# Which second-layer groups lead each chunk of a fused attention and two-layer kernel, and when two additions follow the fifth product

## The chip, the cores and the metric

The kernel runs on one core of a Trainium2 chip. The metric is the device time of one execution in microseconds (us), lower is better. The time before is 329.29 us, the median of three runs (327.78 to 329.35).

## The reference

Causal attention over 8 batches, 8 heads, 576 queries of 64 elements, with 16 additional "beacon" keys that every query sees, and then two dense layers over the 4608 tokens with a leaky ReLU between them:

```
scores = q @ concat(beacon_k, k).T / 8      # queries see only earlier keys, and all beacons
a = exp(scores - max); a /= a.sum()
x = (a @ concat(beacon_v, v)) as [4608, 512]
h = x @ w_in            # [4608, 2048]
g = maximum(0.01 * h, h)
out = g @ w_out         # [4608, 512]
```

## The kernel before

**Attention** goes by pairs of heads, 32 pairs g = 0 to 31, four to a batch. Pairs 0 to 7 are written out by hand as strings of steps. From pair 8 on, `load_natural` (step N, L167) has POOL load q and k, `turn_pair` (step T, L177) has SP issue two transposing DMAs for them, and a `block` (L787) computes 1536 columns of scores: `stretch` (L299) writes them into two one-bank tiles and two two-bank tiles of PSUM, and ACT reads each with Exp (L329, L333) into `aT`. POOL zeroes the triangles (L289). `value` (L374) multiplies by v on PE (L359), in half 0 (12 matmuls) and half 1 (18), and DVE divides by the sums (L388, L389) into `x_nat`. `x_turn` (L412) has SP issue two transposing DMAs that put the pair's 128 columns into `xT`, the input of the first layer.

**The two layers** go by nine chunks of 512 tokens. A first-layer group (`up`, L630, and `moe1`, L431) makes 128 of the 2048 hidden columns of a chunk: four matmuls of 512 columns (L442), one for each quarter j of the 512 inputs; j = 3 needs the last pair of a batch. ACT reads the result with Prelu (L450) into `gT`. There are 16 such groups for a chunk. A second-layer group (`down`, L642, and `moe2`, L524) is eight matmuls of 256 columns (L537). Chunk 0 takes 16 plain groups (L512); each later chunk takes seven products in the order 1, 4, 6, 2, 7, 5, 3 (a Strassen scheme), each in two groups that share a PSUM bank, 14 groups in all. The sums of hidden blocks that products 6, 5 and 3 read are made by DVE (`token_sums`, L469, issued one to a group at L621). After a product's second group, `combine` (L556) reads the bank: ACT copies products 1, 4 and 5 (L568), DVE adds the others (L565), and `store` (L591) has SP send finished blocks out.

In this text **u2.0** is first-layer group 0 of chunk 2, **d1.12** is second-layer group 12 of chunk 1, and **block 7** is the call of `block` with m = 7. The groups d.10 and d.11 of a chunk are product 5; d.12 and d.13 are product 3, the last.

**The order** on each engine is the order in which the Python code issues; nothing reorders it. From pair 8 on a list of events (blocks, values, transposes, loads) is walked in order, and between events `fill` (L603) issues groups, up or down in turn, until the count of groups issued reaches an aim that is spread evenly over the batch. KEPT = 4 groups are held back from each batch's aim, so that four second-layer groups of the old chunk are left when a batch's last pair arrives. At that point `finish` (L685) sets `held` to LEAD = 2: the next two groups are second-layer ones, and they run while the DMA brings the last pair's columns of `xT`. The other two are kept back by the condition with LAST = 2 in `fill`: as long as only two second-layer groups of the chunk are left, first-layer groups go first. With values and blocks left in, the order before around chunk 2 is

```
d1.8 d1.9 d1.10 [value 12, half 1] [x_turn 12] d1.11 (additions of product 5) u2.0 [block 7] u2.1 u2.2 u2.3 [value 13, half 0] u2.4 u2.5 ...
... u2.14 [block 9] u2.15 d1.12 d1.13 [value 15, half 0] d2.0 d2.1 [value 15, half 1] d2.2 ...
```

and around chunk 3

```
d2.10 [block 11] d2.11 (additions of product 5) d2.12 [value 16, half 1] u3.0 u3.1 u3.2 [value 17, half 0] u3.3 u3.4 [block 12] u3.5 d2.13 u3.6 ...
```

Chunks 5 and 6 repeat these two patterns (blocks 20 to 22 and 24 to 25).

**Additions of product 5.** `combine` for product 5 copies the bank by ACT into `p5` and puts two DVE additions and a store into the list `late`. `add_late` (L552), called at the start of every group, issues all that is in the list: so they stand on DVE's queue from the next group on.

**PSUM.** Four of the eight banks form the pool `ps_one` (banks 4 to 7), shared by first-layer groups, products, values and the two one-bank tiles of each block. A bank is given on as soon as its reader is done.

Of the kernel before, what the change touches and what calls it, by code (L numbers as in the profile page):

```python
# [15 lines left out]
def kernel(  # L16
# [487 lines left out]
    def ND(i):  # L504
        return NF if i == 0 else 2 * len(PRODUCTS)
# [18 lines left out]
    def moe2(i, n2):  # L524
        if i == 0:
            moe2_plain(i, n2 // 4, n2 % 4)
            if n2 == NF - 1:
                weight_sums(1)
            return
        n, tile = PRODUCTS[n2 // 2], n2 % 2  # L530
        apart = i == NCH - 1 and n2 >= 10
        if tile == 0 or apart:
            banks["p"] = ps_one.tile([128, 512], FP32, name="acc", tag="one")
        acc = banks["p"]
        lo = 0 if apart else tile * HD
        for fc in range(HF):
            nc.tensor.matmul(  # L537
                out=acc[:, lo : lo + HD],
                lhsT=left(i, n, fc, tile),
                rhs=right(n, fc),  # L540
                start=(lo == 0 and fc == 0),
                stop=(fc == HF - 1),
                skip_group_check=True,
            )
        if apart:
            combine(i, n, acc[:, 0:HD], (tile, tile + 1))
        elif tile == 1:
            combine(i, n, acc, (0, 2))

    late = []  # L550

    def add_late():  # L552
        while late:
            late.pop(0)()

    def combine(i, n, acc, tiles):  # L556
        lo, hi = tiles[0] * HD, tiles[1] * HD

        def part(name, new=False):
            if new and lo == 0:  # L560
                parts[name] = opool.tile([128, 512], FP32, name=name, bufs=1)
            return parts[name][:, lo:hi]

        def add(to, x, y):
            nc.vector.tensor_tensor(out=to, in0=x, in1=y, op=ADD)  # L565

        if n in (1, 4, 5):
            nc.scalar.copy(out=part(f"p{n}", True), in_=acc)  # L568
        if n == 6:
            add(part("u2", True), acc, part("p1"))  # L570
        elif n == 2:
            add(part("p1"), acc, part("p1"))
            store(i, 0, 0, tiles, part("p1"))
        elif n == 7:
            add(part("u3", True), acc, part("u2"))
            add(part("p4"), part("u3"), part("p4"))
            store(i, 1, 0, tiles, part("p4"))
        elif n == 5:
            u2, u3, p5 = part("u2"), part("u3"), part("p5")

            def rest():
                add(u3, u3, p5)
                store(i, 1, 1, tiles, u3)
                add(p5, u2, p5)

            late.append(rest)
        elif n == 3:
            add(part("p5"), acc, part("p5"))
            store(i, 0, 1, tiles, part("p5"))

    def store(i, half, cols, tiles, c):  # L591
        t0 = i * 512 + half * HT + tiles[0] * 128
        n = tiles[1] - tiles[0]
        nc.sync.dma_start(
            out=out[t0 : t0 + n * 128, cols * HD : (cols + 1) * HD].rearrange("(t p) d -> p t d", p=128),
            in_=c.rearrange("p (t d) -> p t d", t=n),
        )

    done1, done2, at2, ready, turn, first_down, held = [0], [0], [0, 0], [0], [0], [0], [0]

    LAST = 2

    def fill(rest=False):  # L603
        i1, fc = divmod(done1[0], NF)
        i2, n2 = at2
        can1 = i1 < ready[0] and (i1 < 2 or i2 > i1 - 2)
        can2 = i2 < NCH and i2 < i1 and done1[0] >= first_down[0]
        if held[0] and can2:
            held[0] -= 1
            down()  # L610
        elif can1 and not (rest and can2) and (turn[0] == 0 or not can2 or (i1 == i2 + 1 and ND(i2) - n2 <= LAST)):
            up()
        elif can2:
            down()
        return can1 or can2
# [14 lines left out]
    def up():  # L630
        i1, n = divmod(done1[0], NF)
        assert i1 < ready[0]
        add_late()
        fc = n if i1 == 0 else n // 2 + n % 2 * HF
        moe1(i1, fc)
        add_due()
        done1[0] += 1
        turn[0] = 1
        if i1 and n % (2 * SLICE) == 2 * SLICE - 1:
            due.extend((i1, op) for op in token_sums(i1, n // 2 + 1 - SLICE, n // 2 + 1))  # L640

    def down():  # L642
        add_late()
        add_due()
        if at2[1] == 4:
            add_all(at2[0])
        moe2(*at2)
        done2[0] += 1
        at2[1] += 1
        if at2[1] == ND(at2[0]):  # L650
            at2[:] = at2[0] + 1, 0
        turn[0] = 0
# [19 lines left out]
            )  # L672

    NG = B * NPAIR
    KEPT, LEAD = 4, 2

    def has(g):
        return 0 <= g < NG
# [68 lines left out]
    with order:  # L747
# [76 lines left out]
        for at, _, what, args in events:  # L824
            while w + 2 < len(ends) and at > ends[w + 1]:
                w, d0 = w + 1, done1[0] + done2[0]
            todo = NF * ready[0] + sum(ND(i) for i in range(ready[0])) - KEPT - d0
            aim = d0 + todo * (at - ends[w]) / (ends[w + 1] - ends[w])
            while done1[0] + done2[0] < aim and fill():
                pass  # L830
            if what is block:
                since = done1[0] + done2[0]
            elif what is value:
                while done1[0] + done2[0] < since + (2 if has_down() else 4) and fill(True):
                    pass
            what(*args)
        while at2[0] < NCH:
            fill()
# [30 lines left out]
```

## Time and profile before

| | us |
|---|---|
| median of three runs | 329.29 |
| lowest and highest | 327.78, 329.35 |
| the profiled execution, its own time | 334.47 |
| span of that execution in the trace | 332.7 |
| PE busy with matmuls | 322.6 |
| ACT busy | 200.7 |
| POOL busy | 185.6 |
| DVE busy | 145.6 |
| 16 DMA engines, mean moved | 120 GB/s |

The profile shows one execution. The profiled one took 334.47 us, 1.77 us of it outside the traced span, and is 5.18 us longer than the median; so times from the trace are compared with the trace's own span. A row of the timeline has the start, the time to the end of the last instruction of the row, the engine (PE matmul, PEld weight load, DVE, ACT, POOL, and SPq for SP's issue of DMAs), the line of the kernel, the operation, output and inputs with shapes, the count, and in brackets the engine's idle time just before and what ended it. Matmuls overlap in the pipeline, so that what counts on PE is the distance from start to start.

### The profile page before, as it was taken

The numbers are of one execution on the slowest core, as the hardware profiler recorded it, in microseconds if no ns is written. First come the engines' busy times: TensorE is split into PE (matmuls) and PEld (weight loads), VectorE is DVE, ScalarE is ACT, GpSimd is POOL, SyncE is SP. The second block draws the span as 40 slices with busy tenths as digits, with TensorE's granted clock in tenths as the row PEclk, the third lists the DMA queues.
The fourth block names the chain that finished last, engine by engine and source line by source line (L and its number), as shares of the span: only waits on it lengthen the run. The fifth ranks groups of instructions, "written<-read, shape, count | busy, mean of one in ns | idle before, by whom it ended". The sixth has DMA issues, their size and how long they took to land.

```text
span 332.7 us, 8488 instructions
## 1 busy us (share of the span) xinstructions
PE 322.6 (97%) x3401; PEld 215.7 (65%) x3429; DVE 145.6 (44%) x297; ACT 200.7 (60%) x336; POOL 185.6 (56%) x354
## 2 busy tenths in 40 slices
PE   8999999999999899999999999999999999999995
PEld 5457456445587457855688888656865695566685
DVE  3327245713565154534434535543553552424344
ACT  3657986197864785477756785686467516643510
POOL 8847874999998568656966887667221000000000
PEclk9999999999999999999999999999999999999999
DMA  7999999999999999999999999999521111000203
GB/s 128 139 181 173 114 195 142 149 179 177 141 140 141 194 133 106 160 145 124 118 138 197 137 146 102 189 106 121 98 97 51 36 52 64 2 33 30 66 32 128
DMA packets 155928, 39.93 MB, mean 120 GB/s; under 512 B 143040, under 2 KB 153152, under 8 KB 155888
## 3 DMA queue, kind: packets, MB, share of 16 engines
q0 software_dynamic: 99824, 18.54, 82.8%
q1 hardware_dynamic: 55792, 20.77, 36.8%
q8 instruction: 27, 0.44, 0.6%
q14 instruction: 13, 0.11, 0.2%
q10 hardware_dynamic: 272, 0.07, 0.1%
HBM read 37.22 MB, written 9.44 MB: 140 GB/s over the span
## 4 chain that ended last, share of the span: by engine, by line
PE 86%; ACT 5%; DMA 4%; DVE 2%; issue 2%; SPq 1%; DVEq 0%; ACTq 0%; POOLq 0%
PE acc L442 34%; PE acc L537 26%; PE av L359 8%; PE sc L314 6%; PE acc L512 4%; PE sc L267 3%; ACT aT L333 3%; DMA xT<-x_nat 2%; PE tp L243 2%; PE av L658 2%; DMA gsum<-in_q_dram 1%; DVE u L565 1%; DVE p L565 1%; ACT aT L329 1%; ACT gT L450 1%
## 5 line engine op out<-in xcount | busy, mean ns | idle before, releaser
L442 PE MATMUL acc<-xT,w_in_sb 128*128 128x512 bf16 (+1 forms) x616 | 134.8, 357 | 3.8 <-DMA xT<-x_nat 1.9
L450 ACT ACTIVATE gT<-acc 128x512 bf16<-128x512 f32 x144 | 83.6, 616 | 54.9 <-PE acc L442 51.1
L289 POOL TENSOR_SCALAR_AFFINE_SELECT aT<-aT 128x256 bf16<-128x256 bf16 (+2 forms) x160 | 61.8, 415 | 66.7 <-ACT aT L329 33.5
L442 PEld LDWEIGHTS <-w_in_sb 128*128 128x128 bf16 x640 | 59.5, 98 | 54.3 <-issue 4.5
L537 PEld LDWEIGHTS <-gT 128*128 128x128 bf16 x512 | 48.8, 98 | 8.3 <-issue 1.2
L333 ACT ACTIVATE aT<-sc 128x1024 bf16<-128x1024 f32 (+3 forms) x64 | 51.8, 896 | 0.0
L537 PE MATMUL acc<-w_out_sb,gT 128*128 128x256 bf16 x384 | 46.2, 273 | 0.1
L359 PEld LDWEIGHTS <-aT 128*128 128x128 bf16 (+1 forms) x960 | 36.8, 98 | 9.0 <-issue 2.6
L537 PEld LDWEIGHTS <-gsum 128*128 128x128 bf16 x384 | 36.8, 98 | 6.7
L359 PE MATMUL av<-v_aug,aT 128*128 128x65 bf16 (+1 forms) x960 | 39.5, 195 | 1.0 <-DVE x_nat L389 0.7
L329 ACT ACTIVATE aT<-sc 128x512 bf16<-128x512 f32 (+3 forms) x64 | 29.0, 522 | 17.9 <-PE sc L314 17.9
L568 ACT COPY p<-acc 128x512 f32<-128x512 f32 (+1 forms) x25 | 14.5, 581 | 38.8 <-PE acc L537 35.2
L388 DVE RECIPROCAL rec<-av 128x6 f32<-128x6 f32 (+1 forms) x64 | 12.0, 187 | 57.9 <-PE av L359 57.6
L171 POOL DMA_DIRECT2D k_nat<-in_k_dram x48 | 34.8, 732 | 0.4
L171 POOL DMA_DIRECT2D q_nat<-in_q_dram x48 | 34.8, 729 | 0.5 <-issue 0.3
L214 POOL DMA_DIRECT2D v_aug<-in_v_dram x40 | 34.2, 858 | 0.2 <-DMA gsum<-in_q_dram 0.2
L389 DVE TENSOR_TENSOR x_nat<-av,rec 128x384 bf16<-128x384 f32 (+1 forms) x64 | 31.4, 491 | 2.2
L276 ACT ACTIVATE aT<-sc 128x1024 bf16<-128x1024 f32 (+3 forms) x32 | 26.7, 875 | 8.8 <-PE sc L267 8.5
L537 PE MATMUL acc<-w_sum,gsum 128*128 128x256 bf16 x256 | 31.9, 273 | 0.0
L621 DVE TENSOR_TENSOR gsum<-gT 128x1024 bf16<-128x1024 bf16 x16 | 11.1, 693 | 30.1 <-ACT gT L450 30.1
L314 PE MATMUL sc<-qT,kT 64*128 64x80 bf16 (+22 forms) x384 | 21.9, 250 | 0.0
L314 PEld LDWEIGHTS <-kT 64*128 64x128 bf16 x384 | 12.8, 94 | 11.6 <-issue 8.1
(62 smaller groups left out, 234.3 us busy)
## 6 DMA issues: line engine op xcount, KB each, us to landing
out_dram<-p SPq DMA_DIRECT2D x26, 256.0 KB, 3.3
q_nat<-in_q_dram POOLq DMA_DIRECT2D x48, 72.0 KB, 5.5
k_nat<-in_k_dram POOLq DMA_DIRECT2D x48, 72.0 KB, 5.3
v_aug<-in_v_dram POOLq DMA_DIRECT2D x24, 128.0 KB, 6.5
w_in_sb<-in_moe_w_in_dram POOLq DMA_DIRECT2D x2, 1024.0 KB, 10.1
w_out_sb<-in_moe_w_out_dram POOLq DMA_DIRECT2D x2, 1024.0 KB, 10.8
out_dram<-u SPq DMA_DIRECT2D x8, 256.0 KB, 3.1
gsum<-in_q_dram POOLq DMA_DIRECT2D x8, 144.0 KB, 5.3
```

Source lines behind the costliest of these rows:

```text
L171: nc.gpsimd.dma_start(out=t[:, :, par], in_=(q, k)[which][b, 2 * hp + par].rearrange("(t p) d -> p t d", p=NR),)
L214: nc.gpsimd.dma_start(out=dst[lo : ROWS[c], c, :, 0:D], in_=v[b, :, OFF[c] : OFF[c] + n].rearrange("h p d -> p h d"),)
L276: nc.scalar.activation(out=aT[:, :, c0 : c0 + w], in_=sc[:, :, 0:w], func=AF.Exp, scale=0.125)
L289: nc.gpsimd.affine_select(out=view, in_=view, compare_op=ALU.is_ge, fill=0.0, base=128 - n if lo == 0 else 0, channel_multiplier=-1, patte ...
L314: nc.tensor.matmul(out=(sc[par] if apart else sc[:, par])[:, at : at + b - a], lhsT=kT[ps_, c * 128 : (c + 1) * 128], rhs=qT[ps_, q0 : q0 ...
L329: nc.scalar.activation(out=probs[g][:, par, lo:hi], in_=sc[par][:, at : at + hi - lo], func=AF.Exp, scale=0.125)
L333: nc.scalar.activation(out=probs[g][:, :, lo:hi], in_=sc[:, :, at : at + hi - lo], func=AF.Exp, scale=0.125)
L359: nc.tensor.matmul(out=avv[:, n, 0 : D + 1], lhsT=aT[0 : ROWS[c], par, a0 : a0 + 128], rhs=va[0 : ROWS[c], c, 2 * hp + par, :], start=(c = ...
L389: nc.vector.tensor_tensor(out=x_nat[:, t0:t1].rearrange("p t e d -> p (t e) d"), in0=avv[:, :, 0:D], in1=rec[:, n0:n1, None].to_broadcast( ...
L442: nc.tensor.matmul(out=acc[:, lo:hi], lhsT=w_in_cols(fc, j), rhs=xT[:, j, x0 : x0 + hi - lo], start=(j == 0), stop=(j == NJ - 1), skip_gro ...
L450: nc.scalar.activation(out=gT[i][:, fc, :], in_=acc, func=AF.Prelu, alpha=0.01)
L537: nc.tensor.matmul(out=acc[:, lo : lo + HD], lhsT=left(i, n, fc, tile), rhs=right(n, fc), start=(lo == 0 and fc == 0), stop=(fc == HF - 1) ...
```

## The change

`LEAD` becomes 4, the same as `KEPT`, so that all four second-layer groups that are left go ahead of the next chunk's first layer. The condition with `LAST` is removed from `fill`. An entry of `late` carries a count of groups, and `add_late` issues it only once that count has passed, which is two groups after the copy instead of one; the last product's `combine` forces what is left, since it adds to the same buffer.

```diff
-    def add_late():
-        while late:
-            late.pop(0)()
+    def add_late(now=False):
+        while late and (now or late[0][0] < done1[0] + done2[0]):
+            late.pop(0)[1]()
...
-            late.append(rest)
+            late.append((done1[0] + done2[0] + 1, rest))
         elif n == 3:
+            add_late(True)
             add(part("p5"), acc, part("p5"))
             store(i, 0, 1, tiles, part("p5"))
...
-
-    LAST = 2
...
-        elif can1 and not (rest and can2) and (turn[0] == 0 or not can2 or (i1 == i2 + 1 and ND(i2) - n2 <= LAST)):
+        elif can1 and not (rest and can2) and (turn[0] == 0 or not can2):
             up()
...
-    KEPT, LEAD = 4, 2
+    KEPT, LEAD = 4, 4
```

The order after it around chunk 2 is

```
d1.8 d1.9 d1.10 [value 12, half 1] [x_turn 12] d1.11 d1.12 [block 7] (additions of product 5) d1.13 u2.0 u2.1 u2.2 [value 13, half 0] u2.3 ...
... u2.12 [block 9] u2.13 u2.14 u2.15 [value 15, half 0] d2.0 d2.1 [value 15, half 1] d2.2 ...
```

and around chunk 3

```
d2.10 [block 11] d2.11 d2.12 [value 16, half 1] (additions of product 5) d2.13 u3.0 u3.1 [value 17, half 0] u3.2 u3.3 [block 12] u3.4 ...
```

The instructions are the same in kind and number. POOL's order is the same. SP's differs in the places of a few stores, and DVE's and ACT's in the places of the additions, sums, copies and Prelus that belong to moved groups.

## The prediction

> **What bounds the kernel now.** I read the busy shares first, then the PE waits, then the PE timeline from start to start around each chunk's beginning.
>
> ```profile
> PE 322.6 (97%) x3401; PEld 215.7 (65%) x3429; DVE 145.6 (44%) x297; ACT 200.7 (60%) x336; POOL 185.6 (56%) x354
> ...
> DMA  7999999999999999999999999999521111000203
> ```
>
> PE is the bound, and the DMA engines are nearly as full until about 230 us. PE's own waits between 80 and 300 us are few:
>
> ```profile
> PE acc L442 <- DMA xT<-x_nat: 1.9, 1, 1.9
> PE av L359 <- DVE x_nat L389: 0.7, 2, 0.4
> PE acc L442 <- ACT gT L450: 0.4, 2, 0.2
> ```
>
> They understate the loss, since a row's end overlaps the next row. From start to start a 512-column matmul takes 0.216 us (12 in 2.59 us), a 256-column one 0.109 (16 in 1.74), so a group takes 0.87 us; value half 0 takes 0.37, half 1 0.56, a block 0.77. What exceeds these is lost time. Around chunk 2's start:
>
> ```profile
> 106.58 0.81 PE L442 MATMUL acc<-xT,w_in_sb 128*128 128x512 bf16 x3
> 109.33 0.38 PE L442 MATMUL acc<-xT,w_in_sb 128*128 128x512 bf16 x1 [1.93 <-DMA xT<-x_nat]
> 109.64 0.83 PE L314 MATMUL sc<-qT,kT 64*128 64x272 bf16 x16
> 110.40 2.77 PE L442 MATMUL acc<-xT,w_in_sb 128*128 128x512 bf16 x11
> 113.00 0.53 PE L359 MATMUL av<-v_aug,aT 128*128 128x65 bf16 x12
> 113.75 2.53 PE L442 MATMUL acc<-xT,w_in_sb 128*128 128x512 bf16 x11 [0.21 <-ACT gT L450]
> ```
>
> u2.0 does three matmuls (0.65 us) and waits for the fourth's columns of xT: 109.33 - 106.58 - 0.65 = **2.10 us** lost. Later, value 13's 12 matmuls take 0.75 instead of 0.37: **0.38** lost, for a bank. ACT shows why:
>
> ```profile
> 109.74 0.60 ACT L450 ACTIVATE gT<-acc 128x512 bf16<-128x512 f32 x1 [2.37 <-PE acc L442]
> 110.23 1.08 ACT L329 ACTIVATE aT<-sc 128x512 bf16<-128x512 f32 x2
> 111.19 2.02 ACT L333 ACTIVATE aT<-sc 128x768 bf16<-128x768 f32 x3
> 113.04 2.37 ACT L450 ACTIVATE gT<-acc 128x512 bf16<-128x512 f32 x4
> ```
>
> The Prelus of the groups behind a block stand behind the block's Exps. Block 7 starts at 109.64; the first Prelu behind it starts 3.40 us later, and PE goes on with its bank at 113.75, 4.1 us behind the block's start; the next follow at a pitch of 0.5 us. With four banks, whatever PE allocates fifth behind a block waits until then. Chunk 5's start repeats the 0.38 (value 25 at 214.82). Chunk 3's start:
>
> ```profile
> 144.14 2.80 PE L442 MATMUL acc<-xT,w_in_sb 128*128 128x512 bf16 x11
> 147.30 0.53 PE L359 MATMUL av<-v_aug,aT 128*128 128x65 bf16 x12 [0.35 <-DVE x_nat L389]
> ```
>
> and DVE in the same stretch:
>
> ```profile
> 145.04 0.84 DVE L565 TENSOR_TENSOR u<-u,p 128x512 f32<-128x512 f32 x1 [3.27 <-ACT p L568]
> 145.91 0.69 DVE L565 TENSOR_TENSOR p<-u,p 128x512 f32<-128x512 f32 x1
> 146.52 0.17 DVE L388 RECIPROCAL rec<-av 128x4 f32<-128x4 f32 x1
> ```
>
> Twelve matmuls (one record is missing) take 147.30 - 144.14 = 3.16 instead of 2.60: **0.56** lost. The two additions of product 5 wait for ACT's copy, which stands behind block 11's Exps, and hold up value 16's division, whose bank value 17 needs; d2.12's bank is idle until d2.13. Chunk 6's start repeats it (245.97 to 249.12, 0.55).
>
> **What the Trainium skill says.** "Perfetto Trace Analysis", section Identifying the Most-Contended Engine: matmul busy share is a poor measure of headroom. The trace agrees: PE reads 97% and these places still lose 2.10 + 2 x 0.38 + 0.56 + 0.55 = 3.97 us. Its section Optimization Strategy takes a repeated gap as a sign that there may be too few PSUM buffers for the next tile; the 0.38 and the 0.56, each seen twice, are such. "TensorE: Matmul & The Clock Gate", Back-to-back issue gap, gives 518 cycles for 512 columns at 2.4 GHz, 0.216 us, as measured. "PSUM — Partial Sum Buffer", Engine vs sequencer instructions: ScalarE's and VectorE's queues are strictly first in, first out. The rows above agree.
>
> **The change part by part.**
>
> *Four groups lead.* At chunk 2's start d1.12 (106.58 to 107.45), block 7 (to 108.2) and d1.13 (to 109.1) now stand ahead of u2.0. Its fourth matmul is due at 109.1 + 0.65 = 109.75, and xT is there at 109.3. Gain 2.10, with 0.4 us of margin. Block 7 itself comes 2.2 us sooner. Its keys (pair 15, issued by SP at 99.25, landing 7.8 us later) are there at 107.05, so nothing; block 8's (pair 16, 107.81 + 6.8 = 114.6) are now due at about 115.9 instead of 118.4, so nothing again. The groups themselves are moved, not added: 2 x 0.87 leave chunk 2's end for every such place.
>
> *Banks behind block 7.* u2.0's Prelu now stands behind the Exps, freed at 107.45 + 4.1 = 111.55; in the built order of banks it is u2.3 that reuses that bank, due at 109.1 + 3 x 0.87 + 0.37 = 112.1. So the 0.38 goes, and at chunk 5 as well: gain 0.76.
>
> *Additions later, last product sooner.* At chunk 3 the division of value 16 goes ahead of the additions, d2.13 follows at once and no bank is idle. Next candidates: the additions end at 145.0 + 2 x 0.72 = 146.4, d2.13's own addition at 147.2, and u3.3, which takes its bank, is due at 144.14 + 4 x 0.87 + 0.37 = 148.0. Gain 0.56, and 0.55 at chunk 6.
>
> *The first layer's end without cover.* This is the cost. Behind block 9 now stand u2.13, u2.14, u2.15, value 15 and d2.0, which takes u2.13's bank: due at 0.77 + 3 x 0.87 + 0.37 = 3.75 us behind the block's start, free at 4.1. **0.35** lost, and the same at d5.0 behind block 22: 0.70. Before, d1.12 took a bank freed ahead of the block. d2.0's eighth matmul needs u2.14's Prelu (4.6), and is due at 4.1 + 0.76 = 4.86: nothing. Bounds: 0, if ACT runs ahead; 1.3 each, if that Prelu and the one for product 4 are late as well by a pitch of 0.5 each. I take 0.35, because the same pattern (three groups and a half value behind block 4) already loses 0.3 at 91.6 us.
> Chunks 3, 4 and 6 end as before; chunks 7 and 8 end with no Exps on ACT, where a Prelu (0.60) keeps up with a group (0.87): nothing. The sums for product 6 are issued two groups later but have four groups (3.5 us) for Prelu and two additions (0.7 + 1.4): nothing.
>
> *Queues.* No DMA is added. SP's stores of product 3 (0.5 us of issue each) go ahead of a transposing pair or two, while SP has idle time between issues; x_turn 16 moves ahead of a store. POOL's order is unchanged. The end of the kernel keeps DVE's and SP's order.
>
> Sum: -2.10 - 0.76 - 1.11 + 0.70 = **-3.3 us**: from 334.47 to 331.2 for the profiled execution. The runs shown are shorter by 5.2 us, and where that lies is not to be seen; if the same places lose the same, the median goes from 329.29 to **326.0**.
>
> **The rivals.** *The DMA wait is moved, not removed.* For it: the DMA row, and that x_turn 11 took 7.5 us against a median of 4.8. Once PE is ahead, block 8 or a later one waits instead; or ordinary runs never had the wait. Against it: 1.3 us of margin at block 8. Then only the bank terms are left: -0.76 - 1.11 + 0.70 = -1.2, 328.1, within 0.5%.
>
> *The uncovered ends cost more than the covered starts bring (slower).* The place is d2.0 and d5.0: bank, last Prelu and product 4's Prelu in a row, 1.3 us each, with the DMA gain absent and half of the bank gains (0.95): -0.95 + 2.6 = +1.7, 331.0. It decides from 1.3 us a place on. Against it: the pitch of 0.5 us between Prelus.
>
> *It doesn't do what it says.* Only chunks 2, 5, 7 and 8 had groups waiting for the first layer's end; at the others only one or two groups move. That is in the sum.
>
> **How the numbers follow.** Forecast 0.67, near 326.0 (324.8 to 327.6: the new waits at 0 give 325.3, a faster base run about 0.5 less, half the DMA gain 327.1). Moved wait 0.23, 327.7 to 329.5. Slower 0.10. Changes of 0.5%, 1.65 us, are about what a measurement of this kernel can tell from none. The range from 324.8 to 328.9 leaves out the slower case and the tail of the second. Faster 0.67, same 0.24, slower 0.09.
>
> **What would show it.** Right: no PE wait for xT; no value row of 12 with 0.75 behind blocks 7 and 20; value 16's reciprocal ahead of product 5's additions; gaps of about 0.35 ahead of d2.0 and d5.0. Wrong: a PE or PEld wait for kT at blocks 7 or 8, or over 1 us ahead of d2.0.

## The result, and the profile after

The changed kernel takes 326.55 us in the median of 13 runs (325.23 to 330.71), the kernel before 328.71 beside it (13 runs, 327.78 to 333.0). The ratio is 0.9935, with a 95% interval of 0.9915 to 0.9956: **2.1 us faster**, 1.4 to 2.8. The ratios here leave out disturbed runs, which the medians contain, so a ratio can differ from that of the medians beside it. The profiled execution of before started its first layer 6.7 us later than the one of after did (31.99 and 25.25 us into the span), so distances inside the spans are compared below, and not the spans. The repeat of before further down, an execution of 327.90 us, starts it at 26.01: of the 6.6 us between these two executions of one kernel, 6.0 lie ahead of the first layer, and so most likely do the 5.2 us that the prediction could not place.

PE stays the bound. The busy row of the page of after:

```profile
PE 317.3 (98%) x3429; PEld 213.4 (66%) x3429; DVE 146.1 (45%) x297; ACT 199.3 (62%) x336; POOL 184.7 (57%) x354
```

PE's waits in after between 80 and 300 us (line waited for, total, times, longest):

```profile
PE acc L537 <- ACT gT L450: 0.4, 2, 0.2
PE av L359 <- ACT gT L450: 0.2, 1, 0.2
```

The row for xT is gone, and so are the two of values for x_nat and the two of first-layer groups for Prelus. New is the first row, two waits of second-layer groups for a Prelu: d2.0 and d5.0. The second row is at 86.20 us, at the value behind block 4, which the prediction named as losing 0.3 before; the repeat of the unchanged kernel has it too. The PE timeline of after at chunk 2's start:

```profile
102.60 1.05 PE L537 MATMUL acc<-w_out_sb,gsum 128*128 128x256 bf16 x8
103.48 2.75 PE L442 MATMUL acc<-xT,w_in_sb 128*128 128x512 bf16 x12
106.07 0.53 PE L359 MATMUL av<-v_aug,aT 128*128 128x65 bf16 x12
106.44 1.89 PE L442 MATMUL acc<-xT,w_in_sb 128*128 128x512 bf16 x8
```

The first row is d1.13, the last group that leads, with d1.12 and block 7 ahead of it; then u2.0 to u2.2 in 106.07 - 103.48 = 2.59 us, the full pace of 12 matmuls; value 13's half 0 takes 106.44 - 106.07 = 0.37, where it took 0.75. Both losses of this place are gone. The end of chunk 2's first layer shows the price, in the PE timeline of after:

```profile
117.51 0.85 PE L314 MATMUL sc<-qT,kT 64*128 64x64 bf16 x16
...
120.90 0.53 PE L359 MATMUL av<-v_aug,aT 128*128 128x65 bf16 x12
121.63 1.91 PE L537 MATMUL acc<-w_out_sb,gT 128*128 128x256 bf16 x16 [0.20 <-ACT gT L450]
```

Behind block 9 come u2.13 to u2.15 and value 15's half 0, and then d2.0 starts 121.63 - 120.90 = 0.73 us behind the value, 0.36 more than the value's 0.37. ACT of after in the same stretch says why:

```profile
120.92 1.64 ACT L450 ACTIVATE gT<-acc 128x512 bf16<-128x512 f32 x3
```

The first Prelu behind the block's Exps starts 120.92 - 117.51 = 3.41 us behind the block, and PE takes that bank at 121.63, 4.12 behind it: the 3.40 and 4.1 that the prediction read behind block 7. What d2.0 waits for there is the bank: its first matmul reads the hidden block that u2.0 made, which was ready long before.

Chunk 3's start, PE of after and then DVE of after:

```profile
137.10 1.89 PE L442 MATMUL acc<-xT,w_in_sb 128*128 128x512 bf16 x8
138.82 0.53 PE L359 MATMUL av<-v_aug,aT 128*128 128x65 bf16 x12
```

```profile
136.42 0.18 DVE L388 RECIPROCAL rec<-av 128x4 f32<-128x4 f32 x1 [2.58 <-PE av L359]
...
137.12 0.84 DVE L565 TENSOR_TENSOR u<-u,p 128x512 f32<-128x512 f32 x1
```

Value 16's division now goes ahead of product 5's additions, and value 17 starts 138.82 - 137.10 = 1.72 us behind the first of eight matmuls: no gap.

**The sum by stages.** From the start of one block to the start of another on PE, and from block 7's start to the end, in us. "The end" means here and below the start of the last product's 16 matmuls, PE's last work; they take the same time in both kernels. Its row in before, and then block 7's and its row in after:

```profile
327.42 1.91 PE L537 MATMUL acc<-w_out_sb,gsum 128*128 128x256 bf16 x16
```

```profile
101.83 0.83 PE L314 MATMUL sc<-qT,kT 64*128 64x272 bf16 x16
...
318.29 1.91 PE L537 MATMUL acc<-w_out_sb,gsum 128*128 128x256 bf16 x16
```


| stage | what it holds | before | after |
|---|---|---|---|
| block 7 to 8 | value 13's bank | 8.21 | 7.85 |
| block 8 to 10 | d2.0 | 15.84 | 16.09 |
| block 10 to 12 | value 17 | 15.80 | 15.24 |
| block 20 to 21 | value 25's bank | 8.21 | 7.85 |
| block 21 to 23 | d5.0 | 15.85 | 16.09 |
| block 23 to 25 | value 29 | 15.79 | 15.24 |
| block 25 to the end | | 76.11 | 76.10 |
| block 7 to the end | | 217.78 | 216.46 |

This total repeats closely: 217.79 in both repeats of the unchanged kernel, 216.47 in the repeat of the changed one. So **1.33 us** of the gain (217.788 - 216.454 before rounding), from block 7 on, is fixed by the order of the instructions. If the runs without a trace share it, what is left of the 2.1 us, about 0.8 (0.1 to 1.5), must lie ahead of block 7; u2.0's wait for xT is there.

One more thing differs there. `LEAD` also acts at chunk 1's start: between the last transposes of x and block 0, after has four second-layer groups (55.95 to 59.70 us), and before has three, with a first-layer group ahead of the third (62.19 to 65.74). From the first layer's first matmul to block 4, the six traces of this document with the old order there take 55.9 to 58.4 us, 57.5 in the mean, and five with the new order 56.9 to 58.4, also 57.5 (the sixth moves block 4 itself). No gain or loss of that place is to be seen, within this spread.

### The profile page after: what moved, and what is told of

Read it like the earlier page. It is cut to its first block, busy times and chain, and to the rows that moved or that the text cites. A ratio compares the mean times of both kernels' runs of the same rounds, so it can differ in the third digit from the quotient of the medians.

```text
span 323.5 us, 8521 instructions
## 1 busy us (share of the span) xinstructions
PE 317.3 (98%) x3429; PEld 213.4 (66%) x3429; DVE 146.1 (45%) x297; ACT 199.3 (62%) x336; POOL 184.7 (57%) x354
## 4 chain that ended last, share of the span: by engine, by line
PE 77%; DMA 10%; POOL 5%; ACT 3%; DVE 2%; issue 2%; DVEq 0%; POOLq 0%; ACTq 0%
PE acc L442 31%; PE acc L537 30%; PE av L359 6%; PE sc L314 6%; DMA w_out_sb<-in_moe_w_out_dram 4%; PE acc L512 4%; DMA w_in_sb<-in_moe_w_in_dram 4%; POOL aT L289 2%; DMA gsum<-in_k_dram 2%; ACT aT L333 2%; POOL gsum L158 2%; ACT aT L329 1%; DVE p L565 0%; ACT gT L450 0%; DVE u L565 0%
## 5 line engine op out<-in xcount | busy, mean ns | idle before, releaser
L289 POOL TENSOR_SCALAR_AFFINE_SELECT aT<-aT 128x256 bf16<-128x256 bf16 (+2 forms) x160 | 59.7, 404 | 51.7 <-ACT aT L329 30.9
L333 ACT ACTIVATE aT<-sc 128x1024 bf16<-128x1024 f32 (+3 forms) x64 | 51.8, 895 | 0.0
L276 ACT ACTIVATE aT<-sc 128x1024 bf16<-128x1024 f32 (+3 forms) x32 | 25.9, 875 | 3.5 <-PE sc L267 3.5
L620 DVE TENSOR_TENSOR gsum<-gT 128x1024 bf16<-128x1024 bf16 x16 | 11.0, 688 | 28.1 <-ACT gT L450 28.1
```

The source lines that it names most:

```text
L276: nc.scalar.activation(out=aT[:, :, c0 : c0 + w], in_=sc[:, :, 0:w], func=AF.Exp, scale=0.125)
L289: nc.gpsimd.affine_select(out=view, in_=view, compare_op=ALU.is_ge, fill=0.0, base=128 - n if lo == 0 else 0, channel_multiplier=-1, patte ...
L333: nc.scalar.activation(out=probs[g][:, :, lo:hi], in_=sc[:, :, at : at + hi - lo], func=AF.Exp, scale=0.125)
```

## The experiments

Two theories stood at the start. The first is the prediction's: fixed gains and losses at banks, which add up whatever the DMA does, and beside them the wait for xT, in ordinary runs perhaps smaller than in the one traced execution. The second: the gain is the wait for xT alone, and the rest of the change does nothing to the time. The first four kernels share one set of runs of before (328.72 us), the next four another (329.16), the last two a third (328.84).

### The kernel before, again

No edit.

> The kernel before, unchanged, for a second trace of it and for the size of the noise. Ratio 1.000 within 0.002. Theory 1 (the DMA wait of u2.0 is a matter of luck, the bank waits are not): the two 0.38 us behind blocks 7 and 20 and the two 0.56 us at chunks 3 and 6 are in this trace too, within 0.05 us, while u2.0's wait for xT lies anywhere from 0 to 2.1 us. Theory 2 (all of the change's gain is the DMA wait): u2.0 waits about 2 us again.

328.69 us, ratio 1.0003 (0.9972 to 1.0034). Its PE timeline at chunk 2's start:

```profile
102.15 1.07 PE L442 MATMUL acc<-xT,w_in_sb 128*128 128x512 bf16 x4
103.16 0.83 PE L314 MATMUL sc<-qT,kT 64*128 64x272 bf16 x16
...
106.52 0.53 PE L359 MATMUL av<-v_aug,aT 128*128 128x65 bf16 x12
107.27 2.10 PE L442 MATMUL acc<-xT,w_in_sb 128*128 128x512 bf16 x9 [0.22 <-ACT gT L450]
```

u2.0 does its four matmuls in one row and the block follows 1.01 us behind its start; the 2.10 us are not there. Value 13 loses 107.27 - 106.52 - 0.37 = 0.38 exactly as before. So the same program has the bank's loss in both executions, and the wait for xT in only one of them.

### The wait for xT alone, taken away

```diff
-                x0 = (at + lo) % (XR * S)
+                x0 = 0 if i == 2 and fc in (0, HF, 1) and j == NJ - 1 else (at + lo) % (XR * S)
```

> The kernel before, but the fourth matmuls of u2.0, u2.1 and u2.2 read columns of xT that were there long ago (so three 128-column blocks of chunk 2's hidden layer are not those of the reference): the wait for x_turn 11 is gone and nothing else is. Theory 1: gain equal to what ordinary runs lose there, 0.9 us if the measured 2.1 us of the change less the 1.2 us of the bank terms is right (ratio 0.997); at most 2.1 us. Theory 2: about 2.1 us, all of the change's gain (0.9935). In the trace no wait of u2.0, and the 0.38 and 0.56 us stay.

Ratio 0.9955 (0.9926 to 0.9984): 1.5 us faster, 0.5 to 2.4. From block 7 to the end it takes 217.79, as before: this edit moves nothing behind block 7. That is an estimate of the wait's worth in ordinary runs, with a wide interval.

### Four groups lead, additions as before

```diff
-        elif can1 and not (rest and can2) and (turn[0] == 0 or not can2 or (i1 == i2 + 1 and ND(i2) - n2 <= LAST)):
+        elif can1 and not (rest and can2) and (turn[0] == 0 or not can2):
...
-    KEPT, LEAD = 4, 2
+    KEPT, LEAD = 4, 4
```

> Half of the change: LEAD = 4 and no LAST condition, the additions of product 5 still in the very next group. Theory 1: the xT wait and the two 0.38 us go, the two 0.35 us at d2.0 and d5.0 come, but value 17 and value 29 still wait about 0.55 us each for a bank whose division stands behind the additions. Net -0.06 us less the DMA wait (0.9): ratio 0.997. Theory 2: as the whole change, 0.9935. A third theory, that the later additions are for nothing and the bank left idle made the 0.56 us: no wait at value 17, ratio 0.9935.

Ratio 0.9963 (0.9938 to 0.9989), 1.2 us faster. Block 7 to 8 is 7.85 us, as in after; block 8 to 10 is 16.09, as in after; block 10 to 12 is 15.93, the loss still there. Its PE timeline at value 17, and then its DVE:

```profile
137.77 1.89 PE L442 MATMUL acc<-xT,w_in_sb 128*128 128x512 bf16 x8
140.05 0.53 PE L359 MATMUL av<-v_aug,aT 128*128 128x65 bf16 x12 [0.39 <-DVE x_nat L389]
140.55 1.67 PE L442 MATMUL acc<-xT,w_in_sb 128*128 128x512 bf16 x7
```

```profile
137.79 0.84 DVE L565 TENSOR_TENSOR u<-u,p 128x512 f32<-128x512 f32 x1 [3.27 <-ACT p L568]
...
139.27 0.17 DVE L388 RECIPROCAL rec<-av 128x4 f32<-128x4 f32 x1
...
139.82 0.68 DVE L565 TENSOR_TENSOR p<-acc,p 128x512 f32<-128x512 f32 x1
```

140.05 - 137.77 - 1.72 = 0.56 is lost, although d2.13 now follows value 16 at once: the additions still go ahead of the reciprocal. The stage is 0.13 longer than before, and that lies right behind value 17: the next group starts 140.55 - 140.05 = 0.50 behind it instead of 0.37, just as d2.13's own addition ends (139.82 + 0.68 = 140.50), which stands behind the two others. From block 7 to the end this half takes 217.83: what it gains at values 13 and 25 it gives back later, mostly at d2.0 and d5.0. So its 1.2 us lie ahead of block 7, where the wait for xT is.

### Additions later, two groups lead

```diff
-        elif can1 and not (rest and can2) and (turn[0] == 0 or not can2):
+        elif can1 and not (rest and can2) and (turn[0] == 0 or not can2 or (i1 == i2 + 1 and ND(i2) - n2 <= 2)):
...
-    KEPT, LEAD = 4, 4
+    KEPT, LEAD = 4, 2
```

(against the changed kernel)

> The other half: the additions of product 5 two groups later, LEAD = 2 and LAST = 2 as before. Theory 1: the two 0.56 us at chunks 3 and 6 go though d2.12's bank stays idle, the xT wait and the two 0.38 us stay, no new wait: -1.1 us, ratio 0.9966. Theory 2: 1.000. The third theory (idle bank): 1.000, with 0.2 to 0.56 us left at value 17.

Ratio 0.9971 (0.9949 to 0.9994): 0.95 us faster, 0.2 to 1.7. From block 7 to the end it takes 216.75, 1.04 less than before, all of it at values 17 and 29 (block 10 to 12: 15.28). PE there:

```profile
138.30 2.80 PE L442 MATMUL acc<-xT,w_in_sb 128*128 128x512 bf16 x12
140.94 0.53 PE L359 MATMUL av<-v_aug,aT 128*128 128x65 bf16 x12
```

Twelve matmuls take 2.64 us, with hardly a loss, and on DVE value 16's reciprocal (138.50) goes ahead of the additions (139.19). In this order d2.12's bank still stands idle until d2.13, as before. **The 0.56 was the additions' place on DVE's queue, and not the idle bank.** And since this half gains without touching the wait for xT, with an interval that ends below 1 (if only just) and 1.04 us in the stages, the second theory falls. The two halves' 1.2 and 0.95 add up to 2.15, the whole change's 2.1, well within their intervals. In the stages they fall short: +0.05 and -1.04 make -0.99 and not -1.33, for the 0.13 us at values 17 and 29 in the first half and 0.04 at the same places in the second go only when both edits are made.

### The changed kernel, again

No edit.

> The changed kernel, unchanged, on the chip of the next three and for a second trace. Ratio to before 0.9935 within 0.003. In the trace: no wait for xT at u2.0, no loss at values 13, 17, 25 and 29, and 0.36 us lost ahead of d2.0 and d5.0, each within 0.05 us.

326.17 us, ratio 0.9921 (0.9897 to 0.9945), 2.6 us faster (1.8 to 3.4), and 216.47 us from block 7 to the end. Less the fixed 1.33, 1.3 us are left for the part ahead of block 7; the first measurement left 0.8.

### Blocks 9 and 22 one group earlier

If d2.0's wait stems from too little work between the block and d2.0, a block that is one group earlier takes it away.

```diff
-            events.append((FIRST + (0.4 if m else 0.6) + 1536 / COLS * m, 2, block, (m,)))
+            events.append((FIRST + (0.4 if m else 0.6) + 1536 / COLS * m - (0.13 if m in (9, 22) else 0), 2, block, (m,)))
```

> The changed kernel with blocks 9 and 22 one first-layer group earlier (and value 14 and 26, half 1, behind the chunk's last group, as the order's rule sets them). Four groups and half a value then stand between the block and the next one in need of a bank. Theory 1 (d2.0 and d5.0 wait for a bank behind the block's Exps): both 0.36 us go, nothing comes: 0.72 us less than the changed kernel, ratio to before 0.9913. Rival (d2.0 waits for the last Prelus that it reads, whatever the banks): the waits stay as they are, 0.9935.

Ratio 0.993 (0.9897 to 0.9963), and 216.29 us from block 7 to the end: only 0.17 less than the changed kernel instead of 0.72. PE:

```profile
117.68 1.13 PE L314 MATMUL sc<-qT,kT 64*128 64x64 bf16 x16
118.74 3.63 PE L442 MATMUL acc<-xT,w_in_sb 128*128 128x512 bf16 x15
122.21 1.09 PE L359 MATMUL av<-v_aug,aT 128*128 128x65 bf16 x30
123.13 1.91 PE L537 MATMUL acc<-w_out_sb,gT 128*128 128x256 bf16 x16
```

d2.0 follows the values without a gap (30 matmuls in 0.92 us, 0.37 + 0.56), but the block itself takes 118.74 - 117.68 = 1.06 us instead of 0.79. The weight loads show what it waits for:

```profile
117.96 0.59 PEld L314 LDWEIGHTS <-kT 64*128 64x128 bf16 x15 [0.19 <-DVE x_nat L389]
```

The edit also put the block ahead of value 14's half 1, and with that its second one-bank tile got the bank of value 14's half 0. DVE was late with that division, since two sums (L620, 0.69 us each, from 115.79) stood ahead of its reciprocal at 117.12; the division ended at 117.91. The wait was exchanged for another one.

### Block 4 as well

The same edit with `m in (4, 9, 22)`; a value behind block 4 lost 0.3 us at 91.6 us in the trace of before.

> As the one above, and block 4 one group earlier as well, where both kernels lose 0.32 us at value 10. Theory 1: 1.04 us less than the changed kernel, ratio to before 0.9903. Rival: 0.9935. Block 4 comes 0.9 us nearer to the landing of its keys: where that is late, its gain of 0.32 us is lost again as a wait of the block.

Ratio 0.9923 (0.9898 to 0.9949), no better than the changed kernel (0.9921 beside it), where 0.9903 was expected. Block 4 now comes ahead of its keys (and of a division, for which it waits 0.30 more). PE:

```profile
76.58 0.67 PE L314 MATMUL sc<-qT,kT 64*128 64x128 bf16 x10 [0.33 <-DMA kT<-k_nat]
```

From block 4 to block 7 takes 20.54 us instead of 19.68: that is one group more in the stage (0.87), and nothing gained.

### Four groups lead at chunk 2 alone

```diff
-        elif can1 and not (rest and can2) and (turn[0] == 0 or not can2 or (i1 == i2 + 1 and ND(i2) - n2 <= LAST)):
+        elif can1 and not (rest and can2) and (turn[0] == 0 or not can2 or (i1 == i2 + 1 and i2 != 1 and ND(i2) - n2 <= LAST)):
...
-            held[0] = LEAD
+            held[0] = 4 if g == 11 else LEAD
```

(against the kernel before)

> The kernel before with all four second-layer groups ahead of chunk 2 alone; chunks 3 to 8 and the additions as before. It takes away u2.0's wait for xT and the 0.38 us of value 13, and brings the 0.36 us ahead of d2.0: what is left of its gain is the wait for xT in ordinary runs. Theory 1: between 0.5 and 1.2 us (ratio 0.9965 to 0.9985), as the six traces have the landing between 0.4 us ahead of u2.0's need and 2.1 us behind it. Theory 2 (all of the gain is that wait): 2.1 us, 0.9935.

Ratio 0.9943 (0.9915 to 0.997), 1.9 us faster (1.0 to 2.8), more than the 0.5 to 1.2 expected, though the interval still touches them. From block 7 to the end it takes 217.92, 0.13 more than before; 0.24 of that is a wait for xT that is left in this execution, so the order alone brings 0.11 there. About 1.8 us (0.9 to 2.7) are then left for the wait that the lead takes away at this one place, with chunk 1's start as before. Its trace has the latest xT of all. PE:

```profile
105.77 3.00 PE L442 MATMUL acc<-xT,w_in_sb 128*128 128x512 bf16 x11
108.61 0.53 PE L359 MATMUL av<-v_aug,aT 128*128 128x65 bf16 x12
```

Twelve matmuls (one record is missing) take 2.84 us: even behind four groups u2.0 waited 0.24. With two groups ahead it would have waited about 2.8 in this execution.

### Blocks 9 and 22 just behind the value

One group earlier again, but behind value 14's half 1 (and 26's), so that the banks come round in another order.

```diff
-            events.append((FIRST + (0.4 if m else 0.6) + 1536 / COLS * m, 2, block, (m,)))
+            events.append((7.632 + m - m // 22 if m in (9, 22) else FIRST + (0.4 if m else 0.6) + 1536 / COLS * m, 6, block, (m,)))
```

> The changed kernel with blocks 9 and 22 one first-layer group earlier, but still behind value 14 and 26, half 1. In the run with the blocks ahead of that half, the 0.36 us at d2.0 and d5.0 went and the blocks themselves took 0.28 us longer, for their one-bank tiles came right behind a group and the value whose banks they take. Here a half value stands between. If banks are all that counts, both 0.36 us go and the blocks take 0.77 us as before: from block 7 to the last matmul 216.46 - 0.72 = 215.75 us. If the last Prelu that d2.0 reads had been next in line, some 0.3 us come back at d2.0's eighth matmul: 216.3. Ratio to before 0.991 within 0.003, not told apart from the changed kernel by time.

325.44 us, ratio 0.9913 (0.9889 to 0.9937), the lowest of all. PE:

```profile
123.21 0.85 PE L314 MATMUL sc<-qT,kT 64*128 64x64 bf16 x16
124.00 3.63 PE L442 MATMUL acc<-xT,w_in_sb 128*128 128x512 bf16 x16
127.46 0.53 PE L359 MATMUL av<-v_aug,aT 128*128 128x65 bf16 x12
127.83 1.91 PE L537 MATMUL acc<-w_out_sb,gT 128*128 128x256 bf16 x16
```

The traced execution took 331.09 us; like the one of before, it started its first layer late (31.86 us into the span), and only distances behind block 7 are read from it. The block takes 0.79, the four groups 3.46, the value 0.37, and d2.0 follows at once. From block 7 to the end it takes 215.74 us, 0.72 less than the changed kernel: both waits of 0.36 are gone, and none came in their place. The times alone would not show this (the intervals overlap with those of the changed kernel); the stages do.

### The kernel before, a third time

No edit.

> The kernel before once more, for another trace of u2.0's wait and the shared chip. Ratio 1.000 within 0.003. The transfer of x_turn 11 lands anywhere from 0.4 us ahead of u2.0's fourth matmul to 2.8 us behind, so a wait of 0 to 2.8 us, with 0.7 the mean of the ten traces so far; from block 7 to the last matmul 217.8 us within 0.1.

328.71 us, ratio 0.9991 (0.997 to 1.0013), and 217.79 us from block 7 to the end. Here u2.0 did not wait for xT, but a value ahead of it waited for v, as the PE timeline shows:

```profile
101.88 0.35 PE L359 MATMUL av<-v_aug,aT 80*128 80x65 bf16 x6 [1.05 <-DMA v_aug<-in_v_dram]
```

From block 4 to block 7 this execution takes 20.95 us, where the first repeat, with hardly a wait for a DMA there, takes 19.72. As this wait came ahead of d1.11, xT landed 1.17 us ahead of u2.0's need, further than the 0.4 expected. So xT is not the only transfer that can hold up PE ahead of block 7; what the change does to this wait, no run shows.

## Why the prediction was right, and what was mis-sized

**The bank terms were right.** The prediction's sum had -0.76 - 1.11 + 0.70 = -1.17 for them; the stages show -1.33. Blocks 7 and 20: -0.36 each, for -0.38. Chunks 3 and 6: -0.56 and -0.55, as said. d2.0 and d5.0: +0.36 each, for +0.35, and the rival that had 1.3 there, and slower, is refuted. Nearly all of the rest: in the trace of before, value 15's half 1 between d2.1 and d2.2 took 131.85 - 131.21 = 0.64 us instead of 0.56, and in after it takes 123.93 - 123.37 = 0.56. The prediction did not look there, so d2.0's stage grew by 0.25 and not by 0.36.

The 0.216 us a matmul, on which these sums rest, holds in after too (12 in 2.59 us). The prediction names the Trainium skill for it, "TensorE: Matmul & The Clock Gate", section Back-to-back issue gap. That section gives the figure for a matmul on its own, and about 131 ns for a stream of them, which no row here shows; the measured 0.216 counts.

**The cause given for chunk 3 was half wrong.** The prediction put the 0.56 down to the additions and to an idle bank, and named the skill's sentence, in "Perfetto Trace Analysis", section Optimization Strategy, that a gap which repeats can mean too little PSUM for the next tile. With the additions moved and the bank still idle, the loss went; with the bank in use and the additions in place, it stayed (0.56). At this gap a change of the queue order was enough, with the same four banks; a pool with more of them was not tried.

**The step that was mis-sized is the -2.10.** The prediction took one execution's wait for xT as that of ordinary runs. What u2.0 waited behind two groups, or would have waited there, is worked out for all twelve traced executions, to about 0.05 us: d1.11's end + 0.65 us, when its fourth matmul is due without a wait, against the landing of xT's last transfer.

| execution | wait, us | to spare, us |
|---|---|---|
| before | 2.10 | |
| before, again | 0.05 | |
| before, a third time (its need came later, for the wait for v) | none | 1.17 |
| the wait taken away | 0.77 | |
| four lead, additions as before | 0.45 | |
| additions later | none | 0.42 |
| after | 0.31 | |
| after, again | none | 0.23 |
| blocks 9 and 22 earlier | none | 0.42 |
| block 4 as well | none | 0.02 |
| four lead at chunk 2 alone | 2.83 | |
| blocks behind the value | 0.47 | |

The mean of the waits is 6.98 / 12 = 0.58 us. The times give more: 0.8 and 1.3 from the two measurements of the change, less 1.33; 1.5 with the wait taken away; 1.2 where four lead; 1.8 at chunk 2 alone, each with an interval of about 0.7 to 1 to either side. So the wait is worth about 1 us in ordinary runs, with 0.6 to 2 open. What is open with it: whether the time measurements contain something else ahead of block 7, where the distance from the first block to block 4 varies between 22.1 and 23.5 us from trace to trace, and where the last trace lost 1.2 us to a wait for v.

So -3.3 became -2.1, and 326.0 became 326.55. That the two times lie so close is in part luck: the kernel before took 328.71 us beside it, 0.58 less than the 329.29 that the prediction started from. The rival that had the wait absent in ordinary runs (328.1) was right on part of the wait, and wrong to leave out the rest. Its other form, a later block that waits in turn, did not come: in after neither block 7 nor block 8 waits for kT.

## What to carry to other kernels

Split a trace's losses into those that every execution has (here those of queue order and buffer rotation, the same in every trace with that order, and priced from one to within 0.1 us each), and those that depend on when a transfer lands, of which one trace is one sample; take two or three executions before the second kind goes into a sum. When a wait is taken away by moving a piece of work, look at which buffer the moved piece gets and who frees it: the same two blocks, moved by the same one group, were worth 0.17 us or 0.72, by their place before or behind one value.

## What the runs showed of the hardware

The same transposing transfer (the second of x_turn 11), at the same place of the program, took from 5.2 to 8.0 us from issue to landing in twelve executions; the DMA row of every page reads 9, 90% busy or more, at this time. The row of xT's two transfers in the kernel with the later additions (least, median, largest), and then the same row in the kernel that leads at chunk 2 alone:

```profile
DMA to landing us min/median/max: 5.2/5.5/5.8
```

```profile
DMA to landing us min/median/max: 7.0/7.5/8.0
```

The second transfer is the least of the two in the first (5.19) and the largest in the second (8.03). The spread of 2.8 us is more than what the change puts ahead of u2.0 (two groups of 0.87 and block 7's 0.77, 2.5 us). Why the transfers of one execution are slower than those of another was not tried.
